# The feature-map folds of a linear-attention kernel in two row tiles of 64 rows

## The chip, the cores and the metric

The kernel runs on one core of one Trainium2 chip. The metric is the device time of one execution in microseconds. Before the change it is 2366.59 us, the median of 3 runs (2366.54 to 2368.55).

## The reference

The input x has 2048 rows of 1024. The output is `g * a + (1 - g) * b`, where g is a sigmoid of a row sum, a is a linear attention with a learned feature map, and b is a gated MLP.

```python
qkv = (x @ wqkv).reshape(B, S, 3, H, Dh)        # H = 32 heads of Dh = 32
pq = einsum("bhsd,hdf->bhsf", q, w_phi)          # one 32 x 32 matrix per head
pk = einsum("bhsd,hdf->bhsf", k, w_phi)
phi_q = concat([softmax(pq), softmax(-pq)], -1)  # and phi_k from pk
kv = einsum("bhsf,bhsd->bhfd", phi_k, v);  z = phi_k summed over s
o = einsum("bhqf,bhfd->bhqd", phi_q, kv) / (einsum("bhqf,bhf->bhq", phi_q, z)[..., None] + 1e-6)
a = o.reshape(B, S, D) @ wo
b = (gelu(x @ w_gate) * (x @ w_up)) @ w_down
g = sigmoid((x * gate_w).sum(-1, keepdims=True))
return g * a + (1 - g) * b
```

All is in float32. What matters here: pq and pk are never computed from q and k. The kernel multiplies the 32 x 32 matrices of `w_phi` into the weights first (`x @ (wq @ w_phi)`); this multiplication of weights is called a fold.

## The kernel before, in words

A product in `float32` stands in the trace as two passes, each a weight load (LDWEIGHTS) and a multiplication (MATMUL); a product in `float32r` as one of each. The large products split each operand into a high and a low `float32r` part and run three products (`PASSES`).

The program has three stages. The first makes keys and values, their features and the sums kv and z, and folds the weights. The second (about 440 us onward) makes the MLP's hidden rows and the queries, and attends. The third (L1190) multiplies with `wo` and `w_down`. The change lies in the first alone, in which the order on TensorE and VectorE is the order of the program text, and the order on ScalarE is made by a scheduler.

The first stage runs over two halves of the heads (`hh`), and in each over 16 row blocks of 128 (`n`, a turn). A turn has two halves of 24 products: keys into the bank `ps[0]`, values into `ps[1]` (`keys_values`, L207). Behind them stands the accumulation of an earlier turn's kv (`accumulate`, L241, 8 products). On VectorE and ScalarE `features` makes the softmax parts `e`, the split values `vs` and the split features `f` (L230 the high part on ScalarE, L236 the low part on VectorE).

A key fold (`fold`, L191) takes a staged block of 128 rows by 512 columns of transposed key weights. Its rows are four heads of 32 for each of four column groups of 128. For each group j it runs one float32 product (L197): the group's 128 x 128 block is the stationary operand, and `bd[:, j]` is the moving one, a 128 x 128 matrix with the four 32 x 32 matrices of `w_phi` on its diagonal and zeros elsewhere. The four results fill one bank of 512 columns, which `split` (L43 on ScalarE, L44 on VectorE) writes as high and low part into the tile `wkv`. The first half's 8 key folds stand at the start of the program, between the first products; their banks come from the pool `pg` (`far_bank`, 4 banks). The second half's 8 stand in the last turn of the first half and use the pool `pd` (`bank`, 4 banks).

A query group's fold (`fold_query`, L140) does the same for 128 query columns (four heads) and all 1024 rows of x's width: 8 blocks of 128. It is cut in two (k = 0 and 1), each with 4 products (L143), one bank and one copy on ScalarE (L145) back into the staged tile. In a turn of the second half, `query_weights(n, 0)` stands between the keys' and the values' products, `query_weights(n, 1)` behind L241; there the tile is stored in `wq_fold` by a DMA on GpSimd's queue, and the next group's matrix `bp` and staged tile are made. The 8 groups go through turns 3 to 10. A turn so takes four banks of `pd`: keys, fold, values, fold.

Of the kernel before, what the change touches and what calls it, by code (L numbers as in the profile page):

```python
# [10 lines left out]
AF = mybir.ActivationFunctionType  # L11
# [5 lines left out]
P = 128  # L17
KC = D // P
NF = DF // P
NG = H // 4  # L20
BLK = 512
# [10 lines left out]
def tile_gated_mix(ctx: ExitStack, tc: tile.TileContext, x, xT, wkT, wqT, wv, w_phi, wo,  # L32
                   w_gate, w_up, w_down, gate_w, out):
    nc = tc.nc
# [7 lines left out]
    def split(dst_h, dst_l, src):  # L42
        nc.scalar.activation(dst_h, src, AF.Copy)  # L43
        nc.vector.tensor_tensor(dst_l, src, dst_h.bitcast(F32), OP.subtract)  # L44
# [10 lines left out]
    def bank():  # L55
        return psum_d.tile([P, BLK], F32, tag="pd", name="pd", bufs=4)

    def far_bank():
        return psum_g.tile([P, BLK], F32, tag="pg", name="pg", bufs=4)
# [17 lines left out]
    wq_fold = [dram.tile([P, KC * P], F32, name=f"wq{g}") for g in range(NG)]  # L77
# [59 lines left out]

        nc.gpsimd.dma_start(dst[m // 4][j, m % 2, :, m // 2 % 2, :], h)

    def fold_query(s, bp, k, pf):  # L140

        for j in range(4):
            nc.tensor.matmul(pf[:, j * P:(j + 1) * P], s[:, (4 * k + j) * P:(4 * k + j + 1) * P],  # L143
                             bp.rearrange("p a b -> p (a b)"), start=True, stop=True)
        nc.scalar.activation(s[:, k * BLK:(k + 1) * BLK], pf, AF.Copy)  # L145


    PE, DVE, ACT, SP = (getattr(mybir.EngineType, n) for n in ("PE", "DVE", "Activation", "SP"))
    with tc.tile_pool(name="kw", bufs=1) as kw, tc.tile_pool(name="kp", bufs=1) as kp, \
# [41 lines left out]
        def fold(hh, kc, bd, s=None):  # L191

            s = staged_pair(hh, kc) if s is None else s
            w = kw.tile([P, 2, 1024], F32R, tag="wkv", name="wkv", bufs=KC)
            pf = bank() if hh else far_bank()
            for j in range(4):
                nc.tensor.matmul(pf[:, j * P:(j + 1) * P], s[:, j * P:(j + 1) * P],  # L197
                                 bd[:, j].rearrange("p a b -> p (a b)"), start=True, stop=True)
            with urgent():
                split(w[:, 0, 512:], w[:, 1, 512:], s[:, 512:])  # L200
                split(w[:, 0, :512], w[:, 1, :512], pf)
            return w

        def keys_values(ps, w, b, t, kc, parts=(0, 1)):
# [80 lines left out]

        staged = []

        def query_weights(n, k):
            if staged:
                g, s, bp = staged[0]  # L290
                fold_query(s, bp, k, bank())
                if k:
                    nc.gpsimd.dma_start(wq_fold[g], s)
                    staged.pop()
            if k and 1 < n < 2 + NG:
                g = n - 2
                bp = kp.tile([P, 4, 32], F32, name="bp", bufs=2)
                nc.vector.tensor_tensor(bp, phi_c[:, g:g + 1, :].to_broadcast([P, 4, 32]), mask, OP.mult)
                staged.append((g, stage((0, 1024, wqT[g])), bp))

        pending, endings, zaccs = [], [], []
        bd, wkv = block_diagonal(0), []
        for hh in range(2):
            chunks = [(b, t) for b in ((0, 1, 2, 3) if hh == 0 else (2, 3, 0, 1)) for t in range(4)]
            ahead = []
            if hh == 0:

                ahead = [[bank(), bank()] for _ in range(2)]
                early = {}
                for step in range(KC):  # L310
                    early["w", step] = w = spare.pop()
                    nc.sync.dma_start(w[:, :512], wkT[hh, step])
                    if step == 0:

                        early["x", 0] = t = spare.pop()
                        nc.sync.dma_start(t[:, :BLK], xT3[:, 0, :BLK])
                    nc.sync.dma_start(w[:, 512:], wv[hh, step])
                    if step == 1:
                        nc.sync.dma_start(early["x", 0][:, BLK:], xT3[:, 1, :BLK])
                    elif step and step % 2 == 0:  # L320
                        early["x", step // 2] = stage((0, 1024, xT3[:, step:step + 2, :BLK]))
                for step in range(KC + LAG):
                    if step < KC:
                        wkv.append(fold(hh, step, bd, early["w", step]))
                        if step % 4 == 0:
                            xb[0, step // 4] = new_quarter(0, step // 4)
                        q = xb[0, step // 4]
                        if step < 2:
                            split(q[:, 0, step], q[:, 1, step], early["x", 0][:, step * BLK:(step + 1) * BLK])
                        elif step % 2 == 0:  # L330
                            split_pair(q, step // 2 % 2, early["x", step // 2])
                    for t, kc in ((0, step - 1), (1, step - LAG)):
                        if 0 <= kc < KC:
                            keys_values(ahead[t], wkv[kc], 0, t, kc)
                gw = kp.tile([P, D], F32, tag="gw", name="gw", bufs=1)
                nc.sync.dma_start(gw, gate_w[None, :].to_broadcast([P, D]))
            for n, (b, t) in enumerate(chunks):
                turn = hh == 0 and n == 15
                if n < len(ahead):
                    ps = ahead[n]  # L340
                else:
                    ps = [bank(), bank() if turn else None]
                    if turn:
                        fresh = []
                        for kc in range(KC):
                            keys_values(ps, wkv[kc], b, t, kc)
                            fresh.append(fold(1, kc, bd))
                            next(steps, None)
                        wkv = fresh
                    else:  # L350
                        for kc in range(KC):
                            keys_values(ps, wkv[kc], b, t, kc, (0,))
                            if hh and n == 1 and kc == 3:
                                finish_z(0, 1, zaccs.pop(), bank())
                        if hh:
                            query_weights(n, 0)
                        ps[1] = bank()
                        for kc in range(KC):
                            keys_values(ps, wkv[kc], b, t, kc, (1,))
                    if len(pending) > 1:  # L360
                        pending.pop(0)()
                    if hh and not turn:
                        query_weights(n, 1)
                    if hh and n == 0:
                        finish_z(0, 0, zacc, bank())
                        zaccs.append(zacc)
                    if hh == 0 and n == 12:
                        bd = block_diagonal(1)
                if n == 0:
                    zacc = kp.tile([P, 2, 16, 32], F32, name="zacc")  # L370
                    pkv = []
                if hh and n == 14:
                    first_w = [weight(w_gate[0]), weight(w_up[0])]
                vs = kp.tile([P, 8, 2, 64], F32R, tag="vs", name="vs", bufs=2)
                f = kp.tile([P, 8, 2, 2, 64], F32R, tag="f", name="f", bufs=2)
                late_steps = steps if hh == 0 and n == 14 else ()
                steps = features(ps, vs, f, zacc, n == 0)
                next(steps)
                for _ in late_steps:
                    pass  # L380
                works = meanwhile(hh, n, chunks)
                for work in works[:1]:
                    work()
                if not (hh == 0 and n == 14):
                    for _ in itertools.islice(steps, 3 if hh == 0 and n == 13 else None):
                        for end in endings[:1]:
                            next(end, None)
                    del endings[:]
                for work in works[1:]:
                    work()  # L390

                def values(hh=hh, pkv=pkv, vs=vs, f=f, n=n):
                    if n == 0:
                        pkv += [psum_g.tile([P, 2, 256], F32, tag="pg", name="pg", bufs=4) for _ in range(4)]
                    accumulate(pkv, vs, f, n == 0, n == 15)
                    if n == 15:
                        endings.append(finish_kv(hh, pkv))

                pending.append(values)
# [678 lines left out]
    with tc.tile_pool(name="op", bufs=1) as op, tc.manual_schedule(engines={PE, DVE, ACT, SP}):  # L1078
# [104 lines left out]
        for n, (turn, d, k, opens, closes) in enumerate(steps):  # L1183
# [3 lines left out]
            for m in range(2):  # L1187
                for c in range(4):
                    for j, (a, e) in enumerate(PASSES):
                        nc.tensor.matmul(ps[c], ls[:, a, m, c * P:(c + 1) * P], rs[:, e, m],  # L1190
                                         start=opens and m == 0 and j == 0, stop=closes and m == 1 and j == 2)
# [5 lines left out]
            while True:  # L1197
                r = todo[len(preps)] if len(preps) < len(todo) else None
                if r and (made_of(r.k) > n or r.when >= n - 1 and needed[r.k] - 2 > n):
                    r = None  # L1200
# [4 lines left out]
                if last_a <= last_r:  # L1205
                    a = waiting[len(adds)]
# [69 lines left out]
```

## Time and profile before

| what | value |
|---|---|
| median of 3 runs | 2366.59 us |
| the profiled execution's own time | 2366.4 us |
| its span, first to last instruction | 2364.6 us |
| TensorE busy (PE) | 2357.6 us |
| weight loads (PEld) | 1958.0 us |
| VectorE (DVE) / ScalarE (ACT) / GpSimd (POOL) busy | 1796.0 / 1077.0 / 141.6 us |
| granted TensorE clock over the span | 1.00 |
| float32 passes of the 16 query folds (L143) | 128 |
| of the first half's 8 key folds (L197 into pg) | 64 |
| of the second half's 8 key folds (L197 into pd) | 64 |

How to read it: a row of the chain or of a group names engine, the written and read tiles, and the line of the kernel; "x8" counts instructions, and for a float32 product each of its passes. Recorded lengths of matrix products overlap, since one starts to stream before the results of the one before it have all been written; the distance from start to start tells what a product costs in a row of them. "[0.18 <-DVE wkv L44]" is idle time of the engine before the instruction, and what ended it.

### The profile page before, as it was taken

The numbers are of one execution on the slowest core, as the hardware profiler recorded it, in microseconds if no ns is written. First come the engines' busy times: TensorE is split into PE (matmuls) and PEld (weight loads), VectorE is DVE, ScalarE is ACT, GpSimd is POOL, SyncE is SP. The second block draws the span as 40 slices with busy tenths as digits, with TensorE's granted clock in tenths as the row PEclk, the third lists the DMA queues.
The fourth block names the chain that finished last, engine by engine and source line by source line (L and its number), as shares of the span: only waits on it lengthen the run. The fifth ranks groups of instructions, "written<-read, shape, count | busy, mean of one in ns | idle before, by whom it ended". The sixth has DMA issues, their size and how long they took to land.

```text
span 2364.6 us, 28504 instructions
## 1 busy us (share of the span) xinstructions
PE 2357.6 (100%) x10625; PEld 1958.0 (83%) x10625; DVE 1796.0 (76%) x2334; ACT 1077.0 (46%) x1388; POOL 141.6 (6%) x266
## 2 busy tenths in 40 slices
PE   9999999999999999999999999999999999999999
PEld 8888888888888888888888888888888888888887
DVE  7877868878888877878788887853574878767773
ACT  4323332455665554656666666653433222223221
POOL 0000000011111111110010000000000000000000
PEclk9999999999999999999999999999999999999999
DMA  5112233545455566574454444533784767978774
GB/s 180 46 45 89 98 116 98 191 170 183 162 184 184 187 211 224 183 272 137 146 177 154 144 151 156 169 125 129 254 289 164 254 235 260 328 256 315 265 266 134
DMA packets 159994, 433.50 MB, mean 183 GB/s; under 512 B 22896, under 2 KB 22896, under 8 KB 159856
## 3 DMA queue, kind: packets, MB, share of 16 engines
q1 hardware_dynamic: 133504, 345.04, 44.1%
q0 software_dynamic: 25312, 86.52, 9.6%
q8 instruction: 83, 1.36, 0.2%
q14 instruction: 55, 0.45, 0.1%
q10 hardware_dynamic: 1040, 0.13, 0.0%
HBM read 336.72 MB, written 94.90 MB: 183 GB/s over the span
## 4 chain that ended last, share of the span: by engine, by line
PE 96%; DVE 1%; DMA 1%; issue 0%; ACT 0%; SPq 0%; POOL 0%; POOLq 0%; ACTq 0%; DVEq 0%
PE po L1190 29%; PE a L793 20%; PE pd L207 15%; PE c L793 13%; PE b L793 7%; PE p L793 7%; PE pg L241 1%; PE misc L995 1%; DMA x<-in_xT 1%; PE pd L110 1%; PE pg L110 1%; PE pd L143 1%; PE pg L197 0%; PE pd L197 0%; DMA x<-q 0%
## 5 line engine op out<-in xcount | busy, mean ns | idle before, releaser
L207 PE MATMUL pd<-wkv,x 128*128 128x512 f32 x1536 | 361.5, 392 | 0.0
L207 PEld LDWEIGHTS pd<-wkv,x 128*128 128x128 f32 x1536 | 284.8, 188 | 58.3 <-issue 1.0
L1190 PE MATMUL po<-tw,wgu 128*128 128x512 f32 x1344 | 309.8, 389 | 0.0
L1190 PEld LDWEIGHTS po<-tw,wgu 128*128 128x128 f32 x1344 | 252.3, 188 | 52.3
L425 ACT ACTIVATE wgu<-stage 128x1024 fp32r<-128x1024 f32 x147 | 155.6, 1059 | 298.8 <-PE po L1190 222.8
L428 DVE TENSOR_TENSOR wgu<-stage,wgu 128x1024 fp32r<-128x1024 f32 x147 | 179.1, 1218 | 117.1 <-ACT wgu L425 116.9
L428 DVE TENSOR_TENSOR tyz<-stage,tyz 128x1024 fp32r<-128x1024 f32 x126 | 153.6, 1219 | 61.1 <-ACT tyz L425 60.9
L793 PE MATMUL a<-x,wgu 128*128 128x512 f32 x744 | 178.9, 389 | 0.2 <-DVE h L769 0.2
L793 PE MATMUL c<-x,tyz 128*128 128x512 f32 x744 | 178.9, 389 | 0.0
L793 PE MATMUL b<-s,tyz 128*128 128x512 f32 x744 | 178.9, 389 | 0.0
L793 PE MATMUL a<-s,v 128*128 128x512 f32 x744 | 178.8, 389 | 0.0
L793 PE MATMUL c<-x,wgu 128*128 128x512 f32 x744 | 178.8, 389 | 0.0
L793 PE MATMUL a<-s,tyz 128*128 128x512 f32 x744 | 178.8, 389 | 0.0
L793 PE MATMUL p<-s,tyz 128*128 128x512 f32 x744 | 178.7, 389 | 0.0
L793 PEld LDWEIGHTS a<-x,wgu 128*128 128x128 f32 x744 | 139.6, 188 | 29.5 <-DVE h L769 0.6
L793 PEld LDWEIGHTS b<-s,tyz 128*128 128x128 f32 x744 | 139.6, 188 | 29.3 <-ACT b L820 0.3
L793 PEld LDWEIGHTS c<-x,tyz 128*128 128x128 f32 x744 | 139.6, 188 | 29.2 <-ACT c L809 0.3
L793 PEld LDWEIGHTS c<-x,wgu 128*128 128x128 f32 x744 | 139.7, 188 | 29.1
L793 PEld LDWEIGHTS a<-s,tyz 128*128 128x128 f32 x744 | 139.7, 188 | 29.0
L793 PEld LDWEIGHTS p<-s,tyz 128*128 128x128 f32 x744 | 139.7, 188 | 29.0
L793 PEld LDWEIGHTS a<-s,v 128*128 128x128 f32 x744 | 139.7, 188 | 29.0
L425 ACT ACTIVATE tyz<-stage 128x1024 fp32r<-128x1024 f32 x126 | 132.9, 1054 | 58.4 <-PE c L793 17.6
(181 smaller groups left out, 3535.7 us busy)
## 6 DMA issues: line engine op xcount, KB each, us to landing
stage<-lm SPq DMA_DIRECT2D x98, 512.0 KB, 3.6
sr<-in_w_down SPq DMA_DIRECT2D x84, 512.0 KB, 5.9
sl<-lm SPq DMA_DIRECT2D x70, 512.0 KB, 4.4
lm<-h POOLq DMA_DIRECT2D x112, 256.0 KB, 2.8
stage<-in_w_gate SPq DMA_DIRECT2D x43, 512.0 KB, 4.2
stage<-in_w_up SPq DMA_DIRECT2D x43, 512.0 KB, 4.1
x<-q SPq DMA_DIRECT2D x128, 128.0 KB, 2.7
stage<-la SPq DMA_DIRECT2D x28, 512.0 KB, 4.2
```

What stands on the lines that cost most here:

```text
L110: nc.tensor.matmul(pg, w[:, a, kc, :], xb[b, kc // 4][:, e, kc % 4, :], start=kc == 0 and i == 0, stop=kc == KC - 1 and i == 2)
L143: nc.tensor.matmul(pf[:, j * P:(j + 1) * P], s[:, (4 * k + j) * P:(4 * k + j + 1) * P], bp.rearrange("p a b -> p (a b)"), start=True, stop ...
L207: nc.tensor.matmul(ps[m], xb[b, kc // 4][:, a, kc % 4, t * P:(t + 1) * P], w[:, e, m * 512:(m + 1) * 512], start=kc == 0 and i == 0, stop= ...
L241: nc.tensor.matmul(pkv[u // 2][:, u % 2], vs[:, u].rearrange("p a c -> p (a c)"), f[:, u].rearrange("p e s c -> p (e s c)"), start=first a ...
L425: nc.scalar.activation(dst, src, AF.Copy)
L428: nc.vector.tensor_tensor(dst, src, dst_h.bitcast(F32), OP.subtract)
L793: nc.tensor.matmul(dst, w[:, h, 4 * part + kc, :], xq[:, e, kc, :], start=first and kc == 0 and i == 0, stop=kc == 3 and i == 2, skip_grou ...
L995: nc.tensor.matmul(po[s], kbs[:, s].rearrange("p a b -> p (a b)"), pts[:, q, s, :], start=q == 0, stop=q == 1)
L1190: nc.tensor.matmul(ps[c], ls[:, a, m, c * P:(c + 1) * P], rs[:, e, m], start=opens and m == 0 and j == 0, stop=closes and m == 1 and j == 2)
```

## The change

The first half's key folds and all query folds are computed in two row tiles. A row tile is the half of the multiplier array that takes 64 of the 128 rows, given by `tile_position=(64 * r, 0)` with operands of 64 partitions. Tile r multiplies rows 64r to 64r + 63 of the stationary block with the 64 x 64 part of the diagonal matrix that holds these rows' two heads; the rest of the matrix in these rows is zero. So a product of 128 rows and 128 moving columns becomes two of 64 rows and 64 moving columns, and tile 0 writes one bank, tile 1 another, 64 columns for each block. The products alternate between the tiles. A float32 product still has two passes.

A query group is folded at one place, behind L241: 16 products into two banks, with two copies of 512 columns on ScalarE that read a bank and write every other 64 columns of the staged tile. A key fold has 8 products into two banks of which 256 columns are used, and two splits of 256 columns in place of one of 512. The second half's key folds stay as they are.

```diff
+    def by_rows(pf, j, s, bd, r):
+
+        rows = slice(64 * r, 64 * r + 64)
+        nc.tensor.matmul(pf[:, 64 * j:64 * j + 64], s[rows], bd[rows, 2 * r:2 * r + 2].rearrange("p a b -> p (a b)"),
+                         start=True, stop=True, tile_position=(64 * r, 0))
+
+    def fold_query(s, bp, pf):
+
+        for j in range(KC):
+            for r in range(2):
+                by_rows(pf[r], j, s[:, j * P:(j + 1) * P], bp, r)
+        for r in range(2):
+            nc.scalar.activation(s.rearrange("p (j r c) -> p r j c", j=KC, r=2)[:, r],
+                                 pf[r].rearrange("p (j c) -> p j c", j=KC), AF.Copy)
...
-            pf = bank() if hh else far_bank()
-            for j in range(4):
-                nc.tensor.matmul(pf[:, j * P:(j + 1) * P], s[:, j * P:(j + 1) * P],
-                                 bd[:, j].rearrange("p a b -> p (a b)"), start=True, stop=True)
+            if hh:
+                pf = bank()
+                for j in range(4):
+                    nc.tensor.matmul(pf[:, j * P:(j + 1) * P], s[:, j * P:(j + 1) * P],
+                                     bd[:, j].rearrange("p a b -> p (a b)"), start=True, stop=True)
+                folded = [(w[:, :, :512], pf)]
+            else:
+                pf = [far_bank() for _ in range(2)]
+                for j in range(4):
+                    for r in range(2):
+                        by_rows(pf[r], j, s[:, j * P:(j + 1) * P], bd[:, j], r)
+                folded = [(w[:, :, :512].rearrange("p a (j r c) -> p r a j c", j=4, r=2)[:, r],
+                           pf[r][:, :256].rearrange("p (j c) -> p j c", j=4)) for r in range(2)]
             with urgent():
                 split(w[:, 0, 512:], w[:, 1, 512:], s[:, 512:])
-                split(w[:, 0, :512], w[:, 1, :512], pf)
+                for part, src in folded:
+                    split(part[:, 0], part[:, 1], src)
...
-        def query_weights(n, k):
+        def query_weights(n):
             if staged:
                 g, s, bp = staged[0]
-                fold_query(s, bp, k, bank())
-                if k:
-                    nc.gpsimd.dma_start(wq_fold[g], s)
-                    staged.pop()
-            if k and 1 < n < 2 + NG:
+                fold_query(s, bp, [bank(), bank()])
+                nc.gpsimd.dma_start(wq_fold[g], s)
+                staged.pop()
+            if 1 < n < 2 + NG:
...
-                        if hh:
-                            query_weights(n, 0)
...
                     if hh and not turn:
-                        query_weights(n, 1)
+                        query_weights(n)
```

The instructions on TensorE at the start of the program (the warm-up products, then key folds into `pg` between products of keys and values into `pd`), first as they stand before, then after the change:

```order
L161 MATMUL pd<-ones 128x128 x7
L197 MATMUL pg<-bd,early 128x128 x8
L207 MATMUL pd<-wkv,x_289 128x512 x6
L197 MATMUL pg<-bd,early 128x128 x4
L207 MATMUL pd<-wkv,x_289 128x512 x6
```

```order
L169 MATMUL pd<-ones 128x128 x7
L143 MATMUL pg<-bd,early 128x64 x16
L225 MATMUL pd<-wkv,x_296 128x512 x6
L143 MATMUL pg<-bd,early 128x64 x8
L225 MATMUL pd<-wkv,x_296 128x512 x6
```

The places are the same; each fold of four products has become one of eight with 64 columns each (line 207 of before is line 225 after the change, 241 is 259). Next, TensorE in the turns with a query fold (`bp` the diagonal matrix, `stage` the staged query weights), before and after:

```order
L241 MATMUL pg<-f,vs 128x256 x8
L143 MATMUL pd<-bp,stage 128x128 x4
L207 MATMUL pd<-wkv,x_993 128x512 x12
L207 MATMUL pd<-wkv,x_1154 128x512 x12
L143 MATMUL pd<-bp,stage 128x128 x4
L207 MATMUL pd<-wkv,x_993 128x512 x12
L207 MATMUL pd<-wkv,x_1154 128x512 x12
L241 MATMUL pg<-f,vs 128x256 x8
```

```order
L259 MATMUL pg<-f,vs 128x256 x8
L143 MATMUL pd<-bp,stage 128x64 x16
L225 MATMUL pd<-wkv,x_1049 128x512 x12
L225 MATMUL pd<-wkv,x_1210 128x512 x12
L225 MATMUL pd<-wkv,x_1049 128x512 x12
L225 MATMUL pd<-wkv,x_1210 128x512 x12
L259 MATMUL pg<-f,vs 128x256 x8
```

The fold between the keys' and the values' products is gone, and the one behind L241 has all 16 products of the group. On ScalarE in the same turns (`vs` the split values, `stage<-pd` the copies of a fold, `f<-e` the high part of the features), before and after:

```order
L43 ACTIVATE vs<-pd 128x8x64
L145 ACTIVATE stage<-pd 128x512
L230 ACTIVATE f<-e 128x8x128
L145 ACTIVATE stage<-pd 128x512
L43 ACTIVATE x_2097<-stage 128x1024
L219 ACTIVATE e<-e 128x1024
```

```order
L43 ACTIVATE vs<-pd 128x8x64
L237 ACTIVATE e<-e 128x1024
L152 ACTIVATE stage<-pd 128x8x64 x2
L248 ACTIVATE f<-e 128x8x128
L43 ACTIVATE x_2161<-stage 128x1024
L237 ACTIVATE e<-e 128x1024
```

The copy that stood behind `f<-e` now stands ahead of it, together with the other one. On GpSimd and SP the order of the instructions is the same before and after.

More of the change, by code (lines that the diff above doesn't have):

```diff
@@ L138, in spill @@
         nc.gpsimd.dma_start(dst[m // 4][j, m % 2, :, m // 2 % 2, :], h)
-    def fold_query(s, bp, k, pf):
-        for j in range(4):
-            nc.tensor.matmul(pf[:, j * P:(j + 1) * P], s[:, (4 * k + j) * P:(4 * k + j + 1) * P],
-                             bp.rearrange("p a b -> p (a b)"), start=True, stop=True)
-        nc.scalar.activation(s[:, k * BLK:(k + 1) * BLK], pf, AF.Copy)
+    def by_rows(pf, j, s, bd, r):
[9 more added lines that the diff above has]
+                                 pf[r].rearrange("p (j c) -> p j c", j=KC), AF.Copy)
     PE, DVE, ACT, SP = (getattr(mybir.EngineType, n) for n in ("PE", "DVE", "Activation", "SP"))
@@ L194, in fold @@
             w = kw.tile([P, 2, 1024], F32R, tag="wkv", name="wkv", bufs=KC)
-            pf = bank() if hh else far_bank()
-            for j in range(4):
-                nc.tensor.matmul(pf[:, j * P:(j + 1) * P], s[:, j * P:(j + 1) * P],
-                                 bd[:, j].rearrange("p a b -> p (a b)"), start=True, stop=True)
+            if hh:
[11 more added lines that the diff above has]
+                           pf[r][:, :256].rearrange("p (j c) -> p j c", j=4)) for r in range(2)]
             with urgent():
                 split(w[:, 0, 512:], w[:, 1, 512:], s[:, 512:])
-                split(w[:, 0, :512], w[:, 1, :512], pf)
+                for part, src in folded:
+                    split(part[:, 0], part[:, 1], src)
             return w
```

## The prediction

> **What bounds the kernel now.** I read the page first, for the shares of the engines and the chain that ended last.
>
> ```profile
> span 2364.6 us, 28504 instructions
> PE 2357.6 (100%) x10625; PEld 1958.0 (83%) x10625; DVE 1796.0 (76%) x2334; ACT 1077.0 (46%) x1388; POOL 141.6 (6%) x266
> ...
> PE 96%; DVE 1%; DMA 1%; issue 0%; ACT 0%; SPq 0%; POOL 0%; POOLq 0%; ACTq 0%; DVEq 0%
> ```
>
> TensorE is busy for 2357.6 of 2364.6 us and carries 96% of the chain. Its busy time contains overlapping records, so I then asked for the windows of the stretches that the change touches (columns: engine busy us, instructions).
>
> ```profile
> 0.00:27.00 27.00, 24.47 (x137) 21.27 (x138) 16.42 (x38) 16.04 (x24) 0.20 (x4) 1.00 0.87 301
> 27.00:190.00 163.00, 163.00 (x769) 136.90 (x768) 134.27 (x167) 49.41 (x55) 0.00 (x0) 1.00 0.17 51
> 250.00:357.00 107.00, 107.00 (x567) 92.05 (x566) 77.56 (x99) 39.15 (x49) 3.87 (x8) 1.00 0.35 114
> 465.00:2364.60 1899.60, 1895.20 (x8353) 1567.82 (x8351) 1422.22 (x1833) 907.88 (x1170) 132.68 (x246) 1.00 0.59 202
> ```
>
> The first 27 us hold the folds of the first half's keys, the stretch from 250 to 357 us the folds of the queries. In the latter TensorE never pauses (107.00 of 107.00), the granted clock is 1.00, and VectorE (77.56) and ScalarE (39.15) have room. In the former it pauses 2.5 us, before its first product. What comes after 465 us is not edited and is TensorE's too; it just starts earlier or later. So the time moves by what TensorE spends more or less on folds, one for one, and by nothing else unless a new wait arises.
>
> What a fold costs now is read from the chain of waits in order of time (start, length, what):
>
> ```profile
> 14.36 0.89 PE pg L197 x8
> 15.25 2.73 PE pd L207 x12
> ...
> 252.11 0.89 PE pd L143 x8
> 253.00 5.46 PE pd L207 x24
> 258.46 0.95 PE pg L241 x8
> 259.41 0.89 PE pd L143 x8
> 260.31 5.49 PE pd L207 x24
> ```
>
> Four f32 products of 128 rows, 128 columns of weights and 128 moving columns stand as 8 passes (the "x8"), each with its own weight load, and take 0.89 us: 0.111 us a pass. There are 16 query folds and 8 key folds of this kind: 16 x 0.89 + 8 x 0.89 = 21.4 us, 0.9% of the span. No edit of the folds can give back more than that.
>
> **Whether a pass is priced by its moving columns or by its weight load** decides the rest.
>
> ```profile
> 221.16 0.86 PE pd L263 x2
> ...
> 8.24 0.30 PEld L207 LDWEIGHTS pd<-wkv,x 128*128 128x128 f32 x2 [0.18 <-DVE wkv L44]
> 8.84 0.30 PEld L207 LDWEIGHTS pd<-wkv,x 128*128 128x128 f32 x2 [0.30 <-DVE x L44]
> 11.81 0.30 PEld L197 LDWEIGHTS pg<-bd,early 128*128 128x128 f32 x2 [0.38 <-DMA early<-in_wkT]
> ...
> L143 PEld LDWEIGHTS pd<-bp,stage x128: 187/192/192, 251.7 to 355.7; 128*128 128x128 f32 x128
> L143 PE MATMUL pd<-bp,stage x128: 270/275/275, 252.0 to 355.8; 128*128 128x128 f32 x128
> ```
>
> Two f32 passes of 512 moving columns take 0.86 us (L263), so 128 columns stream in 0.43 / 4 = 0.107 us. The three rows below it are loads right behind a pause, with nothing queued ahead of them: two loads of 0.19 us lie within 0.30 us, so the second began 0.11 us after the first, as soon as the first was in place. A load of 128 columns of weights therefore also occupies its path for 0.11 us. The two prices are equal, and a pass of 0.111 us is held by both. The change halves one of them (64 moving columns, an estimated 0.054 us) and leaves the other: the stationary block of a tile is still 128 columns wide, with 64 rows instead of 128.
>
> **The change part by part.** *Passes.* A key fold becomes 4 x 2 products, 16 passes instead of 8. A query group, today two folds with 16 passes, becomes 8 x 2 products, 32 passes. Each tile alone still runs 8 passes for a key fold and 16 for a query group. If both tiles load and stream side by side, each at one load of 0.111 us a pass, the fold lasts as long as today: 8 x 0.111 = 0.89 us and 16 x 0.111 = 1.78 us, so 0. No row of this trace shows a tile, so the ends are these: at the top one tile after the other, double, + 8 x 0.89 + 8 x 1.78 = 21.4 us, less 0.4 us that the wait for a load at 11.81 takes in, + 21.0; at the bottom side by side and held only by the moving columns, half, -10.7. I take 0, because the load row is the nearest to what a tile's pass has to do, and because rows 0 to 63 and 64 to 127 read different partitions and write different banks.
>
> The Trainium skill (TensorE: Matmul & The Clock Gate, section on LDWEIGHTS) speaks against a gain: a load's time goes by its columns, and a block with fewer rows takes as long. By it the bottom end drops out and the passes sum to 0 or more; no run here shows a load of 64 rows yet.
>
> *Going into tiles and out again.* Before each group of tile products stands a product over all 128 rows, and after it another. Today the next weights are loaded beside the running product. A product over 128 rows adds down the whole column of the array, a tile ends it at row 63, so I reckon that one has to have left before the other enters.
>
> ```profile
> L207 PE MATMUL pd<-wkv,x x1536: 387/389/799, 7.8 to 414.0; 128*128 128x512 f32 x192
> ```
>
> What that costs can be bounded: a product of 512 columns is recorded with 0.389 us, and the next follows after 5.46 / 24 = 0.228 us, so 0.16 us of each lies under its successor; add the load of 0.11 us that then has no cover: 0.27 us a crossing (275 - 111 ns gives the same 0.16 us on the way out). The lower bound is 0, since today's crossing from L207 to a fold and back adds nothing to the 0.89 us. A gain is excluded here: nothing is spent on a crossing now. There are 7 groups of key folds (the first two folds are adjacent) and 8 query groups, 15 in all, 30 crossings; the first four or so lie where TensorE waits for data anyway, so 26 x 0.27 = 7.0 us. I take the upper value, since a product that must have left is nearest to the rows behind a pause.
>
> The Trainium skill (TensorEngine Tiling, section on key properties) says that changing the tiling mode drains the TensorE, while tiles of one mode can load and multiply in parallel. Taken whole, it would make the passes 0 and the crossings something above 0; neither is shown by a row of this trace.
>
> *One place instead of two.* The fold at k = 0 leaves its place between the two halves of a turn and joins the other behind L241. That saves the crossings of eight more groups, 16 x 0.27 = 4.3 us, which the split form would have paid in tiles; against the kernel before it is 0.
>
> *Evictions.* Each fold is now read from two banks of 256 columns instead of one of 512.
>
> ```profile
> L44 DVE TENSOR_TENSOR wkv<-pg,wkv 128x512 fp32r<-128x512 f32 x8 | 5.5, 690 | 5.1 <-ACT wkv L43 5.1
> L298 DVE TENSOR_TENSOR bp<-phi_c,mask 128x128 f32<-128x128 f32 x8 | 2.3, 285 | 0.0
> L43 ACT ACTIVATE wkv<-pg 128x512 fp32r<-128x512 f32 x8 | 4.8, 598 | 4.8 <-PE pg L197 4.6
> L267 ACT ACTIVATE zb<-pg 32x256 f32<-32x256 f32 x4 | 1.5, 371 | 0.0
> ```
>
> On VectorE 512 columns take 0.69 us and 128 take 0.285, so 256 take about 0.42 by a straight line: two are 0.84, + 0.15 us a key fold. On ScalarE two of 0.37 are + 0.14 us. Only in the first three folds does TensorE wait for a split (0.18 and 0.30 us at 8.24 and 8.84 us), which bounds this at 3 x 0.15 = 0.45 us above and 0 below; I take 0.3. Later the product that uses a folded weight comes 2.73 us after it, which covers 0.3 us. A query group's two evictions stay at 512 columns each, on ScalarE alone. They now stand together ahead of the next f<-e (L230), so that its end, the low part on VectorE (L236) and then L241 are queued behind them:
>
> ```profile
> 277.26 1.06 ACT L230 ACTIVATE f<-e 128x1024 fp32r<-128x1024 f32 x1 [2.64 <-DVE e L227]
> 278.40 1.22 DVE L236 TENSOR_TENSOR f<-e,f 128x1024 fp32r<-128x1024 f32 x1
> ...
> 285.82 0.95 PE pg L241 x8
> ```
>
> L230 had idled 2.64 us and f was complete at 279.6 us, 6.2 us ahead of L241 at 285.8. The fold would end by 273.09 + 1.78 + 0.5 = 275.4, its two evictions of 0.6 us at 276.6, still before 277.26: cost 0, and were it late by 2 us the 6.2 us would cover it.
>
> *Store, banks, queues.* The store of a group's weights waits for the last eviction as before, on GpSimd, with nothing behind it that TensorE needs. A turn still takes four of the four banks, so each is reused a turn (13.7 us) later. The next stage load on SP needs the stage slot about a microsecond later or earlier, with turns between: 0.
>
> **Sum:** passes 0, crossings + 7.0, evictions + 0.3, rest 0: + 7.3 us on the profiled execution's 2366.4 us (span 2364.6 and 1.8 around it; 0.2 under the median of 2366.59): 2373.7 us, + 0.31%.
>
> **The rivals.** *One tile after the other.* If loads of different tiles queue behind one another, a pass costs 0.111 us whatever its tile: + 21.0, with the crossings + 28.3 us: 2394.7; without them 2387.7. For it: none of the rows above has two loads closer than 0.11 us, and each pair of passes in the stream belongs to one tile, so a load of the other has to overtake a waiting product. Against: separate rows and separate banks. A middle form, where a tile's load can't run beside its own product (0.111 + 0.054 = 0.165 us a pass, two tiles abreast, 0.083), gives 8 x (16 x 0.083 - 0.89) + 8 x (32 x 0.083 - 1.78) = + 10.6, with the 7.3: about 2384.
>
> *The crossings are free* and the tiles abreast: + 0.3 to + 2.0 (a fill of 0.11 us for each of 15 groups), 2366.7 to 2368.4, no change that can be told. For it: today's change from f32r to f32 products at the same place costs nothing.
>
> *The halved loads, the side of faster.* If a load's 0.11 us goes with the amount loaded, 64 rows cost 0.056 us; then the moving columns (0.054) decide and two tiles abreast take half: 8 x 0.45 + 8 x 0.89 = -10.7 us. With free crossings that is 2356.0, with crossings at 0.27 us 2363.0. It decides from a pair of passes below 0.111 - 7.3 / 192 = 0.073 us (8 x 8 + 8 x 16 = 192 pairs). For it: a load of half the rows moves half the bytes. Against: if the columns of a block go in one behind the other, all rows of a column at once, the number of rows does not matter.
>
> **How the numbers follow.** About 0.2% (4.7 us) is what a measurement of this kernel can tell from no change: below 2361.9 is faster, above 2371.3 slower. Chances: the forecast 0.34 (its own range 2370 to 2377: crossings at half, or all 30 with a fill of 0.11 us for each of 15 groups); one after the other 0.22; the middle form 0.08; free crossings 0.18; halved loads 0.18, of which 0.14 fall under 2361.9 and 0.04 (dear crossings) above. Faster 0.14; same 0.18 + 0.04 + 0.02 of the forecast's lower edge = 0.24; slower 0.62. The range of 2361 to 2395 leaves out the 0.14 below and holds the rest.
>
> **What would show it.** In the profile after, the chain's rows for the folds (now one line) with 16 passes in the first 27 us and 32 in a query turn: 0.9 + about 0.5 and 1.8 + 0.5 us from the product before to the one behind confirm it; 1.8 and 3.6 mean one after the other; 0.45 and 0.9 mean halved loads. The record behind each group shows whether a crossing idles TensorE: a load that starts only when the product before has ended is right, one beside it makes the crossings free. A new idle time in front of L241's successor, released by ScalarE, would show the order of the evictions as the mistake.

## The result and the profile after

The changed kernel takes 2376.75 us (median of 5 runs) against 2366.59 us before (by now five runs, 2366.47 to 2368.55): ratio 1.0035, 95% interval 1.0024 to 1.0045. It is slower, by a third of a percent. Its five times lie in two groups, a low one of 2371.85 and 2372.30 and a high one of 2376.75, 2377.16 and 2377.74; the profiled run (2377.16 us, span 2375.1) is of the high group, so both have to be explained.

The page of the changed kernel, in the rows that answer to those of before:

```profile
span 2375.1 us, 28921 instructions
PE 2367.1 (100%) x10817; PEld 1962.9 (83%) x10817; DVE 1797.9 (76%) x2342; ACT 1077.0 (45%) x1396; POOL 142.2 (6%) x266
```

TensorE still fills the span. There are 192 more multiplications, as there should be: 8 x 8 for the key folds and 8 x 16 for the queries. The chain of waits in the turns with query folds (start, length, what; L225 is the old L207, L259 the old L241):

```profile
241.81 10.91 PE pd L225 x48
252.72 0.95 PE pg L259 x8
...
265.53 1.93 PE pd L143 x32
267.46 11.11 PE pd L225 x48
```

A turn without a fold has 48 products in 10.91 us; one behind a tile group has them in 11.11. A query group therefore costs 1.93 + 0.20 = 2.13 us. Before, it cost two folds of 0.89, and its 48 products took 5.46 + 5.49 = 10.95: 1.82 us. So + 0.31 us a group, 2.5 us for 8. The 32 passes are not twice as long as 16 were.

The start of the program is another matter (L169 is the warm-up):

```profile
2.50 3.35 PE pd L169 x14
5.85 3.61 PE pg L143 x32
9.46 2.86 PE pd L225 x6
12.32 1.90 PE pg L143 x16
14.22 2.86 PE pd L225 x6
17.08 1.32 PE pg L143 x16
18.40 1.59 PE pd L225 x6
19.99 1.04 PE pg L143 x16
21.03 2.96 PE pd L225 x12
```

The same fold takes 1.90 us at 12.3, 1.32 at 17.1 and 1.04 from 20.0 on, and the same six products 2.86 and then 1.59 us. The groups of weight loads in the windows 9.4 to 16.9 us and 18.4 to 30 us show more (count, busy us, mean ns of one); the last row is the warm-up of the kernel before, at 2.4 to 5.4 us:

```profile
L225 PEld LDWEIGHTS pd<-wkv,x 128*128 128x128 f32 x12 | 3.6, 323 | 1.0
L143 PEld LDWEIGHTS pg<-bd,early 64*128 64x128 f32 x16 | 1.8, 325 | 0.7 <-issue 0.7
...
L225 PEld LDWEIGHTS pd<-wkv,x 128*128 128x128 f32 x36 | 6.4, 188 | 1.5
...
L161 PEld LDWEIGHTS pd<-ones 128*128 128x128 f32 x14 | 3.1, 330 | 2.5 <-DVE ones L156 2.5
```

A load of 0.188 us is recorded with 0.32 us until about 17 us, as in the warm-up, where both kernels have 0.33 us: in this run TensorE worked at half speed up to there. In the kernel before, the loads after 7.8 us are recorded with 0.19 us, as in the rows of the prediction.

The granted clock that the views print does not show this: it is 1.00 from the start, also in the prediction's first window, because a stretch for which the trace has no entry counts as full speed. The list of granted clocks in the trace's file has its first entry, full speed, at 17.63 us after the change and at 5.91 us before it. Later there is no entry of less than full speed until the last 2.3 us of the span.

### The profile page after: what moved, and what is told of

The parts are those of the page before. It is cut to its first block, busy times and chain, and to the rows that moved or that the text cites. A ratio compares the mean times of both kernels' runs of the same rounds, so it can differ in the third digit from the quotient of the medians.

```text
span 2375.1 us, 28921 instructions
## 1 busy us (share of the span) xinstructions
PE 2367.1 (100%) x10817; PEld 1962.9 (83%) x10817; DVE 1797.9 (76%) x2342; ACT 1077.0 (45%) x1396; POOL 142.2 (6%) x266
## 4 chain that ended last, share of the span: by engine, by line
PE 99%; DVE 1%; DMA 0%; issue 0%; SPq 0%; ACT 0%; ACTq 0%
PE po L1205 29%; PE a L808 21%; PE pd L225 15%; PE c L808 14%; PE b L808 7%; PE p L808 7%; PE pg L259 1%; PE misc L1010 1%; PE pd L110 1%; PE pg L110 1%; PE pd L143 1%; PE pg L143 0%; PE pd L206 0%; DMA stage<-in_w_gate 0%; PE pd L169 0%
## 5 line engine op out<-in xcount | busy, mean ns | idle before, releaser
L225 PE MATMUL pd<-wkv,x 128*128 128x512 f32 x1536 | 362.0, 394 | 0.0
L225 PEld LDWEIGHTS pd<-wkv,x 128*128 128x128 f32 x1536 | 286.9, 189 | 60.0 <-issue 1.0
```

Source lines behind the costliest of these rows:

```text
L225: nc.tensor.matmul(ps[m], xb[b, kc // 4][:, a, kc % 4, t * P:(t + 1) * P], w[:, e, m * 512:(m + 1) * 512], start=kc == 0 and i == 0, stop= ...
```

## The experiments

The theory after the result: tiles run abreast at one load a pass, so the passes cost nothing; each group of tile products pays for going in and out, about 0.31 to 0.36 us; and the tile folds at the start can delay the moment at which the clock goes from half to full speed (the "late clock"). The rivals: the loss lies in the place of the fold or in the order of ScalarE's copies; a tile's pass is itself dearer; the slow start comes from chance in the transfers or from the doubled evictions. In the experiments "before" has medians of 2366.78, 2366.63 and 2366.71 us in the three series of runs. Edits are given against the changed kernel, or against the run that is named.

**Queries only in tiles.**

```diff
-            if hh:
-                pf = bank()
+            if True:
+                pf = bank() if hh else far_bank()
```

> Query folds in tiles, key folds whole as before. Theory: a query group costs 0.31 us more (start to start in the trace after), 8 groups give + 2.5 us, and the start of the program is that of before: 2369.0 us, its runs within 1.5 us of each other. Rival (the loss lies in the start alone): 2366.6. Rival (the slow start comes from chance in the transfers, not from the tiles): two groups of times 5 us apart here too.

Measured: 2369.87 us (11 runs, 2369.38 to 2370.31), ratio 1.0012 (1.0003 to 1.0021): + 3.1 us, and one group. Over the turns with query groups the trace falls behind by 2.46 us, as expected. The rest lies in instructions that are the same: 0.37 us in the first 47 us (the first accumulation begins at 46.92 us, before at 46.55), and 0.3 us in the second stage, whose length (first product into `a` to first of the third stage) is 1212.3 us before and 1212.6 here, and 1212.0 in the run without any tiles below. So nothing ties these 0.7 us to the tiles.

**Keys only in tiles**, the queries whole and at one place.

```diff
-            for r in range(2):
-                by_rows(pf[r], j, s[:, j * P:(j + 1) * P], bp, r)
+            nc.tensor.matmul(pf[j // 4][:, j % 4 * P:(j % 4 + 1) * P], s[:, j * P:(j + 1) * P],
+                             bp.rearrange("p a b -> p (a b)"), start=True, stop=True)
... (the two copies: one of each bank, whole)
```

> Key folds in tiles; query folds whole, at one place. Theory: the warm key folds cost 0.36 us each (8 x 0.36 = 2.9 at most, so 2369 to 2369.5), and in those runs in which the products at the start stay at half speed until about 17 us some 5 us more (2374). So two groups of times, about 5 us apart. Rival (the query groups make the difference between runs): one group of times.

Measured: median 2370.20 us, ratio 1.0015 (1.0006 to 1.0024); nine runs between 2368.79 and 2371.43, two at 2374.15 and 2374.45. The high group is there, though rarer than in the changed kernel (2 of 11 against 3 of 5, from the same code at the start). The profiled run is of the low group. Its chain:

```profile
2.11 5.28 DMA early<-in_wkT
...
7.44 1.11 PE pg L143 x16
...
27.34 1.04 PE pg L143 x16
28.38 20.63 PE pd L224 x90
49.01 0.95 PE pg L258 x8
```

The first accumulation (L258 here) begins at 49.01 us. In the kernel before and in the profiled run of the changed one, the chain has

```profile
46.55 0.95 PE pg L241 x8
```

```profile
33.00 20.63 PE pd L225 x90
```

so that it begins at 46.55 and at 33.00 + 20.63 = 53.63 us. So the start is 2.46 us later with key folds in tiles, and half speed puts another 4.62 us on top. Not all of the 2.46 us is the tiles': the second fold starts in both runs when its transfer lands, here at 7.44 us and before at 6.87, and from there to the first accumulation the difference is 41.57 - 39.68 = 1.89 us. In the run at half speed TensorE does not wait there, so half speed may be worth up to 4.62 + 0.57 = 5.2 us; the two groups of the changed kernel lie 5 us apart.

**The first two key folds whole**, all others in tiles.

```diff
-            if hh:
-                pf = bank()
+            if hh or kc < 2:
+                pf = bank() if hh else far_bank()
```

> As the changed kernel, but the first two key folds whole, so that the first full-speed window is filled by products over 128 rows as before. Theory of the late clock: all runs near 2371.5 (+ 2.5 for the queries, + 6 x 0.36 = 2.2 for the keys), and the loads at 12 to 17 us recorded with 0.19 us, not 0.33. Rival (the slow start comes from doubled evictions or transfers): still two groups, up to 2377.

Measured: 2372.25 us, all 11 runs between 2371.49 and 2372.96, ratio 1.0021 (1.0012 to 1.003). The loads from 9.4 to 16.9 us, in the same windows as above:

```profile
L225 PEld LDWEIGHTS pd<-wkv,x 128*128 128x128 f32 x18 | 3.1, 188 | 0.7
L143 PEld LDWEIGHTS pg<-bd,early 64*128 64x128 f32 x48 | 2.9, 188 | 1.1 <-issue 0.7 <-DMA early<-in_wkT 0.4
```

Six of the eight folds are in tiles, with their doubled evictions and the same transfers, and the high group is gone. This trace alone shows little, since its list of clocks has full speed from 5.67 us, before any tile product. The counts say more: 5 of 16 runs in the high group with tiles right behind the warm-up, none of 22 (these and the last experiment's 11) with two whole folds between.

The lists also give a reason for the chance, though only one run of the high group has a trace. In every trace the stretch at full speed lasts a multiple of 3.413 us (2355.20 us after the change are 690 of them, 2358.61 us before 691), so the clock is set anew in steps of that length, which don't begin with the program. Counted back from 17.63 us, the steps of the changed kernel's run begin at 0.57, 3.98, 7.39, 10.80 and 14.22 us. They hold 1.48 and 1.87 us of warm-up, then 1.34, 1.52 and 2.86 us of products over 128 rows (by the rows of its chain above), and only the last is followed by full speed. With the keys only, the step from 3.01 to 6.42 us holds some 2.8 us of warm-up, and full speed follows. So the same 3.35 us of warm-up are enough or not by where a step begins. With the first two folds whole, the first tile comes at 9.55 us, 7 us behind the start of the warm-up, and in 7 us there is always one whole step.

**No tiles, one place.** Both edits of the first two experiments together.

> No tiles at all: query folds whole but at one place, with two banks and the two copies together. Theory (the place costs nothing): 2366.6, within 0.1%. Rival (the two copies ahead of the features, or the bank order, cost the time): 2369.

Measured: 2366.39 us, ratio 0.9998 (0.9989 to 1.0007). The place of the fold and the order of the copies cost nothing; the rival falls.

**Two places, in tiles.** From "queries only": the group's 16 products are cut in two again, 8 between keys and values, 8 behind the accumulation, into the same two banks.

```diff
-        for j in range(KC):
+        for j in range(4 * k, 4 * k + 4):
...
+                        if hh:
+                            query_weights(n, 0)
                         ps[1] = bank()
...
```

> Key folds whole; query folds in tiles, but cut in two again: 8 products between keys and values, 8 behind the accumulation, into the same two banks, copies at the end. Same tile passes as with queries only in tiles, 16 groups of tile products instead of 8. Theory (the loss is the crossing into tiles and out, 0.31 us a group): + 16 x 0.31 = 4.9 us, 2371.5, that is 2.5 above the kernel with queries only. Rival (a tile pass itself is dearer): no difference to queries only, 2369.0.

Measured: 2372.84 us (2371.80 to 2373.37), ratio 1.0025 (1.0015 to 1.0034), 3.0 us above "queries only", where 2.5 was expected. The chain:

```profile
260.06 1.04 PE pd L143 x16
261.10 5.66 PE pd L227 x24
266.76 1.04 PE pd L143 x16
```

Half a group's passes cost 1.04 + (5.66 - 5.46) = 1.24 us, 0.35 more than a whole fold's 0.89, and twice as many groups cost twice as much: + 6.2 us against + 3.1. The price hangs on the groups, not on the passes.

**One tile after the other.** From "queries only": the loops over r and j are swapped.

```diff
-        for j in range(KC):
-            for r in range(2):
+        for r in range(2):
+            for j in range(KC):
                 by_rows(pf[r], j, s[:, j * P:(j + 1) * P], bp, r)
```

> Key folds whole; in a query group all 8 products of tile 0 first, then all 8 of tile 1. Theory (a tile's pass is priced by its load, and only neighbours of different tiles run abreast): 32 passes of 0.11 = 3.6 us a group instead of 1.8, + 14.2 + 2.5: 2383. Rival (loads of the other tile are pulled ahead over any distance): 2369 as with the alternating order. Rival (a tile's pass costs its moving columns, 0.054): 2369 too, but with passes 0.054 apart.

Measured: 2392.91 us (4 runs, 2387.78 to 2393.64), ratio 1.0106 (1.0092 to 1.0119), 10 us above what was expected. The chain of the profiled run (2387.78 us), and its windows (columns: window, busy us, then the clock before the last two numbers):

```profile
258.70 3.32 PE pd L143 x32
262.02 12.71 PE pd L225 x48
...
275.68 3.32 PE pd L143 x32
...
326.62 3.32 PE pd L143 x32
329.94 11.11 PE pd L225 x48
```

```profile
255.00:258.70 3.70, 3.70 (x22) 3.10 (x20) 3.70 (x7) 1.07 (x1) 0.00 (x0) 1.00 0.00 0
258.70:262.40 3.70, 3.70 (x34) 3.59 (x35) 3.63 (x6) 1.89 (x3) 0.00 (x0) 1.00 0.38 100
262.55:265.85 3.30, 3.30 (x9) 2.62 (x8) 3.27 (x4) 1.65 (x3) 0.67 (x1) 0.50 0.44 179
266.00:274.00 8.00, 8.00 (x37) 6.61 (x36) 3.62 (x5) 2.12 (x2) 0.00 (x0) 1.00 0.26 69
...
L225 PEld LDWEIGHTS pd<-wkv,x 128*128 128x128 f32 x8 | 2.6, 329 | 0.8
```

The last row is the group of loads at 262.6 to 265.8 us, at a granted clock of 0.50: recorded with 0.33 us, as at the start of the changed kernel.

The first theory's passes are there: they no longer run abreast (3.32 us for 32, 0.104 each), and both rivals are out. A group costs 3.32 + 0.20 - 1.82 = 1.70 us more than before, 13.6 us for 8. The rest is the clock: behind this group of one-tile passes, in which TensorE never paused, the granted clock is 0.50 for about 3.4 us, at the cost of 12.71 - 11.11 = 1.6 us. It happened behind four of the eight groups in this run: 13.6 + 4 x 1.6 = 20.0 of its 21.2 us. The other three runs have no trace, but their mean granted clocks of 0.994 to 0.995, against 0.997 here, stand for seven or eight such stretches (13.6 + 8 x 1.6 = 26.4 us; the median is 26.3 above).

In the list of clocks the four stretches begin at 262.46, 279.53, 296.60 and 313.66 us and last 3.41 us each, with 13.65 us, four steps, between them. The step that ends at 262.46 began at 259.05, so 2.97 us of it are one-tile passes. Worked out in the same way for the eight groups, the four steps behind which the clock fell hold 2.73 to 2.97 us of them, and those of the other four groups at most 2.67.

**Half the moving columns.** From "queries only": one head a tile.

```diff
-        nc.tensor.matmul(pf[:, 64 * j:64 * j + 64], s[rows], bd[rows, 2 * r:2 * r + 2].rearrange("p a b -> p (a b)"),
+        nc.tensor.matmul(pf[:, 64 * j:64 * j + 32], s[rows], bd[rows, 2 * r],
... (the copies: these 32 columns alone)
```

> Key folds whole; query folds in tiles with 32 moving columns instead of 64 (the second head of each tile is left out of the folded weights). Theory (priced by the load): no change against queries only, 2369.0, pairs of passes 0.112 us apart. Rival (priced by the moving columns): half, - 8 x 0.9 = - 7, 2362.

Measured: 2369.72 us, ratio 1.0013 (1.0004 to 1.0022), the time of "queries only" (2369.87). The 32 passes take 1.90 us where 64 moving columns took 1.93:

```profile
258.80 1.90 PE pd L143 x32
260.71 11.11 PE pd L225 x48
```

**Half the weight columns.** From "queries only".

```diff
-        nc.tensor.matmul(pf[:, 64 * j:64 * j + 64], s[rows], bd[rows, 2 * r:2 * r + 2].rearrange("p a b -> p (a b)"),
+        nc.tensor.matmul(pf[:64, 64 * j:64 * j + 64], s[rows, :64], bd[rows, 2 * r:2 * r + 2].rearrange("p a b -> p (a b)"),
... (the copies: these 64 partitions alone)
```

> Key folds whole; query folds in tiles with a stationary block of 64 columns instead of 128 (the second half of each block's rows of the weights is left unfolded). Theory (priced by the load, and the load by its columns): a load of 64 columns costs 0.056, the pairs of passes come 0.056 to 0.07 apart, - 8 x 0.7 to 0.9 against queries only: 2362 to 2363.5. Rival (some other floor of 0.11 a pair): 2369.

Measured: 2362.54 us, ratio 0.9982 (0.9973 to 0.9991). The chain:

```profile
258.85 1.08 PE pd L143 x32
259.93 11.11 PE pd L225 x48
```

The same 32 passes take 1.08 us in place of 1.93. Moving columns can be halved for nothing, weight columns give 0.85 us a group: a tile's pass is priced by its load, and the load by its columns.

**A longer warm-up**, from the changed kernel.

```diff
-        for _ in range(7):
+        for _ in range(16):
             nc.tensor.matmul(warm[:, :P], ones, ones, start=True, stop=True)
```

> The changed kernel with 16 products of ones ahead of the first fold instead of 7 (their result is not used). Theory of the late clock: at least one whole window of full-width work lies ahead of the first tile, so that no run stays at half speed: all runs within 1.5 us of each other, at 2372 to 2373 (the changed kernel's low group, plus up to 1.5 us by which the longer warm-up may delay the first fold). Rival (the slow group comes from transfers or evictions): two groups, up to 2378.

Measured: median 2375.17 us (5 runs, 2373.91 to 2376.11), ratio 1.0037 (1.0023 to 1.005). The chain of its profiled run:

```profile
8.05 1.93 PE pg L143 x32
...
30.04 20.63 PE pd L225 x90
```

The first two folds take 1.93 us together, full speed, and there are no two groups of times. But the time is 2 to 3 us above the forecast, and the spread of 2.2 us wider: the added products end only at 8.05 us, so that the first accumulation begins at 30.04 + 20.63 = 50.67 us, 1.66 us later than with "keys only". The forecast already allowed 1.5 us for this. The low group's 2372.1 + 1.66 = 2373.8 us fits the profiled run (2373.91, the shortest of the five); why the other four are 1.2 to 2.2 us longer stays open. As a cure it is no good, and as a test it supports the late clock less sharply than the two whole folds do.

**Four tiles.** The runs above point to it: what has to shrink is the load. From "queries only", each row tile's block is cut into two column tiles; all of the result is made.

```diff
-        nc.tensor.matmul(pf[:, 64 * j:64 * j + 64], s[rows], bd[rows, 2 * r:2 * r + 2].rearrange("p a b -> p (a b)"),
-                         start=True, stop=True, tile_position=(64 * r, 0))
+        for c in (0, 64):
+            nc.tensor.matmul(pf[c:c + 64, 64 * j:64 * j + 64], s[rows, c:c + 64],
+                             bd[rows, 2 * r:2 * r + 2].rearrange("p a b -> p (a b)"),
+                             start=True, stop=True, tile_position=(64 * r, c))
```

> Key folds whole; query folds in four tiles of 64 rows by 64 weight columns, each row tile's block cut into two column tiles that write partitions 0 to 63 and 64 to 127 of the same bank: 64 passes a group with loads of 64 columns, the whole result. Theory (tiles of different columns load abreast too): 16 x 0.067 = 1.08 us a group as in the run with 64 weight columns, 2362.5, 4 us below the kernel before. Rival (loads for the same rows queue): 64 loads, two abreast, 32 x 0.056 = 1.8 us, 2369.8 as with two tiles.

Measured: 2362.39 us (11 runs, 2361.76 to 2363.43), ratio 0.9983 (0.9974 to 0.9992): 4.3 us faster than the kernel before. The chain, and the group of its 512 loads:

```profile
258.72 1.09 PE pd L144 x64
259.81 11.11 PE pd L227 x48
```

```profile
L144 PEld LDWEIGHTS pd<-bp,stage x512: 129/135/135, 258.6 to 351.6; 64*64 64x64 f32 x171
```

64 passes take 1.09 us, that is 0.068 us for each 4 abreast; the loads of 64 columns are recorded with 0.135 us where those of 128 have 0.188.

**Four tiles for the keys too**, from the third fold on (the edit above, on "the first two key folds whole").

> As four tiles for the queries, and the key folds from the third on in four tiles too. Theory: a key fold of 0.89 us becomes 8 x 0.067 = 0.54 and pays 0.36 for its crossings, so within 0.1 us each of the whole fold: 2362.5 to 2363.5. Rival (loads queue): 2372, as with two tiles and the first two folds whole.

Measured: 2362.55 us (2361.14 to 2363.51), ratio 0.9982 (0.9973 to 0.9991). No difference to four tiles for the queries alone, as forecast: a key fold is so short that the shorter passes only pay for its crossings.

## Why the prediction was right, and what in it was not

**Passes: 0.** Right, and for the reason given. The change halved the moving columns and left the load; 32 passes in pairs take 16 x 0.111 = 1.78 of the 1.93 us. The three runs that separate the prices (32 moving columns, 64 weight columns, one tile after the other) each came out on the side of the load, so the rival of halved loads and that of one tile after the other are both out: a load of 64 rows costs what one of 128 rows costs (0.104 us a pass with one tile at a time, 0.111 before), and two run abreast if they alternate. One sum on the way is a little off: the middle form comes to + 10.5, not + 10.6, which leaves its "about 2384" as it is. The rule of the Trainium skill that spoke against a gain (TensorE: Matmul & The Clock Gate, section on LDWEIGHTS: time by columns, not rows) is borne out by 1.93 against 1.08 us.

**Crossings: + 7.0.** The mechanism was right, the term too large. Two places of the timeline of the changed kernel, into the tiles and out:

```profile
265.25 0.28 PE L259 MATMUL pg<-f,vs 128*128 128x256 f32 x1
265.45 0.18 PEld L143 LDWEIGHTS pd<-bp,stage 64*128 64x128 f32 x1
...
267.18 0.28 PE L143 MATMUL pd<-bp,stage 64*128 64x64 f32 x2
...
267.39 0.30 PEld L225 LDWEIGHTS pd<-wkv,x 128*128 128x128 f32 x2
```

The load does wait: before the change the next load goes beside the running product, this one starts 0.20 us after the start of the last product. But it does not wait for all of it, as the prediction had reckoned ("has to have left"): that product's record ends at 265.25 + 0.28 = 265.53 us, and the load starts 0.08 us ahead of this (ends of products are modelled). A product in that row is followed by the next after 0.95 / 8 = 0.12 us, so 0.08 us is lost and not 0.16; on the way out 0.21 - 0.11 = 0.10. With the load of 0.11 us that has no cover, as predicted, that is 0.19 and 0.21, and the last tile pass gives back an estimated 0.05 us by which it is shorter than its place. Together this is an estimate of 0.35 us a group; the turns show 0.31, the key folds 0.36 (1.04 + 2.95 against 0.89 + 2.74), so 0.15 to 0.18 a crossing where 0.27 was taken. For 8 query groups that is 2.46 us, and for the start, evictions included, 1.9 to 2.46 us (keys only): 4.4 to 4.9 us where the prediction had 7.3. The Trainium skill's sentence on draining at a change of the tiling mode (TensorEngine Tiling, key properties) agrees with the row at 265.45 in kind.

**Evictions: + 0.3.** The halves cost what the straight line gave:

```profile
L43 ACT ACTIVATE wkv<-pg x8: 377/382/387, 18.4 to 29.3; 128x256 fp32r<-128x256 f32 x8
L44 DVE TENSOR_TENSOR wkv<-pg,wkv x8: 412/420/426, 18.9 to 29.8; 128x256 fp32r<-128x256 f32 x8
```

How much of it reached TensorE cannot be told from the crossings at the start; it is within the 2.46 us. Of the two waits that bounded the term, only the one of 0.18 us is for a folded weight; by its own row that of 0.30 us at 8.84 is for the split of x.

**One place, copies, store: 0.** Right (0.9998 without tiles).

**The clock: not in the sum at all.** The prediction took the granted clock as given because it stood at 1.00, which at the start says nothing. In the profiled run half speed up to 17.6 us cost 4.6 us or a little more, and it fits the two groups of times: 4.4 to 4.9 us of tiles alone would be 2371.0 to 2371.5, near the low group's 2372; the high group is 5 us above. The other two runs of the high group have no trace, so that they too had the late clock is inferred. So the forecast of + 7.3 lies between the groups, and it is near the measured + 10.2 partly by luck: one term was 2.4 to 2.9 us too large, and one of 4.6 was missing. Some 0.7 us more appear in the second stage (1212.9 us long after the change, 1212.3 before), in the same instructions; over all the profiled runs, with tiles or without, this stage takes 1212.0 to 1213.7 us.

## What to carry to other kernels

Before cutting a product into tiles, find out whether the load or the moving columns price a pass: rows fewer than 128 saved nothing on a load here, so row tiles alone can at best break even where a float32 pass moves as many columns as it loads. Cut the weight columns too (here 4.3 us faster than before, where two row tiles were 3.1 us slower), alternate the tiles, and put all tile products of a group at one place, since every group paid about 0.3 us for going in and out. Keep tile products out of the first microseconds of a program, until some 7 us of full-width products have run, and don't trust the printed clock there.

## What the runs showed of the hardware that was not expected

TensorE can be busy without a pause and still lose its clock. Behind 3.3 us of passes of one 64-row tile at a time the granted clock fell to 0.50 for 3.41 us, with no pause before it. Behind the alternating tiles it didn't, but these last 1.93 us, less than the 2.67 us of one-tile passes in a step behind which it didn't fall either; so whether two tiles abreast count for more is open. At the start, full-width warm-up products for 3.4 us followed by tile products left TensorE at half speed until 17.63 us in one profiled run; with two full-width folds between, no run has such a time. The Trainium skill (TensorE: Matmul & The Clock Gate, part 1) says that the clock is decided in free-running windows of about 3.4 us by how busy TensorE was. The traces agree: the half-speed stretches last 3.41 us, the full ones multiples of it, and the steps fall at other places of the program from run to run, which fits that the same code is slow in some runs only. That a partly used array counts for less was not tried apart from these runs.

Four tiles of 64 by 64 load abreast, also the two that share the same 64 rows: 64 loads, recorded with 0.135 us each, in 1.09 us.
